# A fused attention and mixture kernel: first products copied by ScalarE into the second's bank, one pooled sum instead of three, and attention, loads and x sums moved in time

## The chip, the cores and the metric

The kernel runs on one core of a Trainium2 chip. A core has a matrix engine (TensorE, "PE" in the profile; its weight loads are "PEld"), a vector engine (DVE), a scalar engine (ScalarE, "ACT"), GpSimd ("POOL") and a sync engine (SP) that mostly issues DMAs. The metric is device time in microseconds (us) of one execution. The kernel before takes 514.0 us in the median of its first three runs (513.14 to 515.52), and the profiled execution spans 511.7 us. All executions quoted here are marked fast. Medians of several chips and sets of runs are quoted, so the ratio to the kernel before, timed in the same rounds, is the number to compare.

## The reference

```python
# attention: batch 8, heads 8, sequence 576, head size 64
k_p, v_p = mean of k, v over groups of 8 tokens              # 72 keys and values
attn = softmax(q @ k_p.T / 8);   attn_out = attn @ v_p
x = attn_out as (8*576, 512)                                  # 4608 tokens
# mixture: 4 experts, hidden size 1024
p = domain_probs / (domain_probs.sum(-1) + 1e-9)
out = sum over e of p[:, e] * (relu(x @ w1[e]) @ w2[e])
```

## The kernel before

The tokens are worked in nine chunks: 512 tokens of each of the eight batches, and one chunk with the remaining 64 of every batch. Chunk 0 is special; it ends near 78 us. Chunks 1 to 8 run in steady state: one expert of a chunk takes seven slots, and each slot holds three products, one of each "unit" of the up projection and one of the down projection of the expert before. Each seven-product scheme computes what eight plain block products would. It pays with sums on DVE: of weights once, of x once per chunk ("x sums", tile xs), of the hidden layer once per expert ("hidden sums", tiles S and H).

Some names in what follows: PSUM is the memory that PE writes its products to; a "bank" here is a tile of 128x512 fp32 in it. A "relu sum" is the DVE instruction that adds a PSUM bank and a copy and takes the relu. xT and kpT are the transposed tokens and the transposed pooled keys, made by DMA transposes. An "x_tok buffer" holds the tokens before their transpose.

```python
# up projection: seven products into two PSUM banks of a unit
bank, grows, lhs, rhs = [
    (0, False, b11, a11),
    (1, False, b21, a12),
    (0, True, t[:, 1], s[:, 1]),
    ...
][step]
...
if step == 0 or step == 3:
    nc.scalar.copy(out=part[:, 0], in_=ps)
elif step == 2:
    nc.scalar.copy(out=part[:, 1], in_=ps)
elif step == 1:
    relu_sum(quarter(0, 0), ps, part[:, 0])        # DVE: relu(PSUM + copy)
elif step == 4:
    relu_sum(quarter(1, 1), ps, part[:, 0])
elif step == 5:
    nc.scalar.activation(out=quarter(0, 1), in_=ps, func=ACT.Relu)
else:
    relu_sum(quarter(1, 0), ps, part[:, 1])

# down projection: each step's block is scaled by a probability and added to acc
if step in pooled and e > 0:                        # pooled = (1, 4, 6)
    for j in range(BLOCKS):
        nc.scalar.activation(out=addend[:, j], in_=ps[:, j], func=ACT.Copy, scale=prob)
    nc.gpsimd.tensor_add(out=dst, in0=dst, in1=addend[:])   # one addend tile only
else:
    for j in range(BLOCKS):
        add(ps[:, j], c, e, row * BLOCKS + j, cols, first)  # DVE, or ScalarE when first

# chunk 0: loads in the GpSimd queue
load_w2(1); load_w1(3); load_w2(2); load_w2(3)
...
# attention of batch b is computed inside chunk b-1: division on DVE into x_tok
# (three buffers), then a DMA transpose x_tok -> xT, then x_sums(b) on DVE
x_tok = npool.tile([P, 2, NPAIR, D], BF16, name="x_tok", bufs=3)
...
put(26, lambda: x_sums(b))
```

The softmax here doesn't subtract the row's maximum and nothing guards it: scores larger than these inputs give would overflow.

Of the kernel before, what the change touches and what calls it, by code (L numbers as in the profile page):

```python
# [10 lines left out]
ALU = mybir.AluOpType  # L11
# [6 lines left out]
def kernel(  # L18
# [54 lines left out]
    wu_bf = wpool.tile([P, E, 3, HK, FH], BF16, name="wu_bf")  # L73
    wt_bf = wpool.tile([P, E, 3, HF, HD], BF16, name="wt_bf")
    acc = const.tile([P, NR, DM], F32, name="acc")
    x_rem = const.tile([P, NPAIR, NT], BF16, name="x_rem")
    ident = const.tile([P, P], BF16, name="ident")
    partial = const.tile([P, 2, 2, NT], F32, name="partial")
# [106 lines left out]
    def combine(dst, a, op, b):  # L185
        nc.vector.tensor_tensor(out=dst, in0=a, in1=b, op=op)  # L186
# [64 lines left out]
    def idle(n):  # L251

        w_ps = work_bank()
        for _ in range(n):
            nc.tensor.matmul(w_ps, lhsT=zeros[:, 0:P], rhs=zeros)  # L255

    def fold_values(b, hs):
        raw = raw_v if b >= BUSY else raws[("vraw", b)]
# [213 lines left out]
    def x_sums(c):  # L472
        a11, a21, a12, a22 = x_parts(c)
        s = state[("xs", c)] = xpool.tile([P, 3, HK, HN], BF16, name="xs")
        combine(s[:, 0], a21, ALU.add, a22)
        combine(s[:, 1], s[:, 0], ALU.subtract, a11)
        combine(a21, a11, ALU.subtract, a21)
        combine(s[:, 2], a12, ALU.subtract, s[:, 1])

    def relu_sum(dst, ps, part):  # L480
        nc.vector._custom_dve(TENSOR_ADD_SAT, out=dst, in0=ps, in1=part, s0=LARGEST, s1=0.0)  # L481
# [1 line left out]
    def up_product(c, e, unit, step):  # L483
        b11, b21, t3, b22 = weight_parts(e)
        a11, s3, a12, a22 = x_parts(c)
        t, s = wu_bf[:, e], state[("xs", c)]
        bank, grows, lhs, rhs = [
            (0, False, b11, a11),
            (1, False, b21, a12),
            (0, True, t[:, 1], s[:, 1]),  # L490
            (0, True, t3, s3),
            (1, False, t[:, 0], s[:, 0]),
            (0, True, t[:, 2], a22),
            (1, True, b22, s[:, 2]),
        ][step]
        ps = units[unit][bank][:]
        for n in range(2):
            for kc in range(HK):
                f = (2 * unit + n) * P
                nc.tensor.matmul(  # L500
                    ps[:, n * HN:(n + 1) * HN], lhsT=lhs[:, kc, f:f + P], rhs=rhs[:, kc, :],
                    start=(not grows and n == 0 and kc == 0), stop=(kc == HK - 1),
                    skip_group_check=True,
                )
        part = partial[:, unit]
        H_sb = hidden[(c, e)]

        def quarter(f, tok):
            return H_sb[:, f, tok, 2 * unit:2 * unit + 2, :].rearrange("p i n -> p (i n)")

        if step == 0 or step == 3:
            nc.scalar.copy(out=part[:, 0], in_=ps)  # L512
        elif step == 2:
            nc.scalar.copy(out=part[:, 1], in_=ps)  # L514
        elif step == 1:
            relu_sum(quarter(0, 0), ps, part[:, 0])
        elif step == 4:
            relu_sum(quarter(1, 1), ps, part[:, 0])
        elif step == 5:
            nc.scalar.activation(out=quarter(0, 1), in_=ps, func=ACT.Relu)  # L520
        else:
            relu_sum(quarter(1, 0), ps, part[:, 1])



# [24 lines left out]
    def down(c, e, step, flip=0, pooled=()):  # L550
# [2 lines left out]
        a11, a12, a21, a22 = quarters(c, e)  # L553
        chain, grows, lhs, rhs, row, col, first = [
            lambda: (0, False, a11, w[:, LO, 0:HD], 0, 0, True),
            lambda: (1, False, a12, w[:, HI, 0:HD], 0, 0, False),
            lambda: (0, True, S2, t[:, 1], 0, 1, True),
            lambda: (1, False, a21, t[:, 0], 1, 1, True),
            lambda: (0, True, S3, w[:, LO, HD:DM], 1, 1, False),
# [10 lines left out]
                    skip_group_check=True,  # L570
                )
        cols = slice(col * HD, (col + 1) * HD)
        if step in pooled and e > 0:
            for j in range(BLOCKS):
                prob = p_all[:, c * NR + row * BLOCKS + j, e:e + 1]
                nc.scalar.activation(out=addend[:, j], in_=ps[:, j], func=ACT.Copy, scale=prob)  # L576
            dst = acc[:, row * BLOCKS:(row + 1) * BLOCKS, cols]
            nc.gpsimd.tensor_add(out=dst, in0=dst, in1=addend[:])  # L578
        else:
            for j in range(BLOCKS):  # L580
                add(ps[:, j], c, e, row * BLOCKS + j, cols, first)
# [78 lines left out]
    make_identity(nc, ident[:])  # L660
    every = slice(0, H)

    def pieces_first():

        at = {}

        def put(s, i, *pieces):
            at.setdefault((s, i), []).extend(pieces)
# [17 lines left out]
        for r in range(NR):  # L686
            put(2, 3 + r, lambda r=r: context(1, r))
            put(2, 4 + r, lambda r=r: turn(1, r))
        put(3, 1, lambda: load_part(2, 1))
        put(3, 3, lambda: load_q(2))  # L690
        put(3, 5, lambda: load_part(2, 2))
        put(3, 7, lambda: x_sums(1))
        return at

    def pieces_at(b):

        at = {}

        def put(slot, piece):
            at.setdefault(slot, []).append(piece)  # L700

        if b < B:
            late = b == BUSY
            put(4 if late else 0, lambda: queries(b))
            put(5 if late else 0, lambda: fold_keys(b, every))
            put(6 if late else 1, lambda: keys(b, every))
            put(7 if late else 5, lambda: fold_values(b, every))
            for pair, slot in enumerate((9, 11, 12, 13) if late else (6, 8, 12, 13)):
                put(slot, lambda pair=pair: scores(b, pair))
            for r in range(NR):  # L710
                put((14, 16, 19, 21)[r], lambda r=r: context(b, r))
                put((15, 17, 20, 22)[r], lambda r=r: turn(b, r))
            put(26, lambda: x_sums(b))
            if late:
                put(1, lambda: load_part(b, 3))
                put(2, lambda: load_q_rem(b))
            if b + 1 < B:
                put(8 if late else 6, lambda: load_part(b + 1, 0))
                put(9 if late else 8, lambda: (load_q(b + 1), load_q_rem(b + 1)))
                put(12, lambda: load_part(b + 1, 1))  # L720
                put(17, lambda: load_part(b + 1, 2))
                put(22, lambda: load_part(b + 1, 3))
        if b % 2 == 0 and b <= B:
            i = b // 2 - 1
            put(0, lambda: rem_queries(i))
            put(4, lambda: rem_scores(i))
            put(7, lambda: rem_context(i))
            put(8, lambda: rem_turn(i))
        if b == B:
            put(12, lambda: x_sums(B))  # L730
        return at

    ENG = mybir.EngineType
    with tc.manual_schedule(
# [11 lines left out]
        load_whole(1, k, "kraw")  # L746
        load_q(1)
        load_whole(1, v, "vraw")
        load_w2(1)
        load_w1(3)  # L750
        load_w2(2)
        load_w2(3)
        load_q_rem(0)
# [1 line left out]
        load_part(2, 0)  # L755

        first_pieces = pieces_first()

        for s, (above, below) in enumerate(
                [((0, 1), None), ((0, 2), (0, 0)), ((0, 3), (0, 1)), (None, (0, 2))]):  # L760
            if s == 1:
                hidden_sums(*below, 0)
                hidden_sums(*below, 1)
            for i in range(FCH):
                if above:
                    up(*above, (i,))
                if below and s != 1 and i % 2:
                    down_plain(*below, i // 2)
                if s == 1 and i < 7:
                    down(*below, i)  # L770
                    if i in (1, 2):
                        hidden_sums(*below, i + 1)
                for piece in first_pieces.get((s, i), ()):
                    piece()
        psum_first.__exit__(None, None, None)
        psum_last = ctx.enter_context(
            tc.tile_pool(name="psum_last", bufs=1, space=bass.MemoryType.PSUM))
        units[0] = [psum_last.tile([P, NT], F32, name=f"unit0{i}") for i in range(2)]



        N = len(order)
        below_of = [(0, 3)] + order
        sums = {}
        for at, pieces in (((2, 3, 4, 5), first_weight_sums(2)), ((9, 10, 12, 13), weight_sums(2)),
                           ((16, 17, 18, 19), first_weight_sums(3))):
            sums.update(zip(at, pieces, strict=True))
        POOLED = (1, 4, 6)
        for g in range(7 * N + 1):
            t, i = divmod(g, 7)  # L790
            if t < N:
                up_product(*order[t], 0, i)
            t2, i2 = divmod(g - 1, 7)
            if 0 <= t2 < N:
                up_product(*order[t2], 1, i2)
            if g >= 1:
                down(*below_of[t2], i2, t2 % 2, POOLED)
            if i < 4 and t < N:
                hidden_sums(*below_of[t], i)
            if t < N:  # L800
                c = order[t][0]
                at = pieces_at(c + 1)
                for piece in at.get(g - 7 * E * (c - 1), ()):
                    piece()
            if g in sums:
                sums[g]()
            if g == 7 * (N - 2):
                load_last_weights()
        down_last(*order[-1])
# [28 lines left out]
```

## Time and profile before

| what | number | where it is read |
|---|---|---|
| PE busy, whole span | 97% of 511.7 us | page, part 1 |
| PE in the chain of waits | 79% | page, part 4 |
| PE busy 150 to 300 us | 149.62 of 150 us | windows |
| PE busy 50 to 60, 80 to 95, 95 to 120, 120 to 150 us | 7.87, 12.97, 22.97, 27.60 us | windows |
| DVE busy 120 to 150 us | 29.03 of 30 us | windows |

The page of the kernel before begins with each engine's busy time, its share of the span and its number of instructions:

```profile
PE 495.1 (97%) x4578; PEld 406.6 (79%) x4578; DVE 405.1 (79%) x776; ACT 291.7 (57%) x557; POOL 181.4 (35%) x160
```

The windows view of the kernel before gives, for each stretch, its length and the busy time of PE, PEld, DVE, ACT and POOL (instructions in brackets), then granted clock, DMA share and GB/s:

```profile
50.00:60.00 10.00, 7.87 (x44) 2.79 (x42) 3.81 (x6) 4.71 (x8) 0.00 (x0) 0.83 1.25 205
80.00:95.00 15.00, 12.97 (x138) 10.46 (x137) 14.24 (x27) 7.82 (x15) 6.10 (x5) 1.00 0.92 112
95.00:120.00 25.00, 22.97 (x223) 19.14 (x222) 22.46 (x44) 15.48 (x28) 11.36 (x10) 1.00 0.80 94
120.00:150.00 30.00, 27.60 (x258) 23.72 (x255) 29.03 (x54) 15.29 (x31) 11.34 (x9) 1.00 0.61 61
150.00:300.00 150.00, 149.62 (x1460) 129.44 (x1460) 127.41 (x247) 93.78 (x179) 68.12 (x56) 1.00 0.72 83
```

The last row is the most important for judging the change: after 150 us PE has nothing to gain. PE's loss between 50 and 150 us shows in the first four rows.

PE's timeline of the kernel before around 54 us (start, duration, what, and in brackets the idle time before it and what ended it):

```profile
51.21 0.39 PE L299 MATMUL att<-qT,kpT 64*128 64x256 bf16 x4
53.73 1.56 PE L448 MATMUL unit<-xT,w_bf 128*128 128x512 bf16 x4 [2.13 <-DMA w_bf<-in_moe_w_dram]
55.22 0.61 PE L299 MATMUL att_first<-qT,kpT 64*128 64x256 bf16 x4
55.76 1.89 PE L448 MATMUL unit<-xT,w_bf 128*128 128x512 bf16 x4
```

PE waits 2.13 us for a weight load. The four matmuls after it take 1.56 and 1.89 us, where the same four take 1.03 us at 50.25 us, at a granted clock of 1.00: the granted clock of the 10 us from 50 to 60 is 0.83 on average, and 0.50 from 54.1 to 57.5 us.

The wait list of the kernel before names what else stops PE later (in total, times, longest):

```profile
PE unit L448 <- DMA w_bf<-in_moe_w_dram: 2.1, 1, 2.1
DVE xs L186 <- DMA xT<-x_tok: 2.1, 2, 1.4
PE att L299 <- DMA kpT<-kp: 2.0, 1, 2.0
PE o_ps L567 <- DVE S L186: 1.6, 3, 1.0
PE unit L500 <- DVE H L481: 1.2, 2, 0.9
```

And the groups that the change touches (line, engine, operation, count, busy us, mean ns of one):

```profile
L481 DVE CUSTOM_DVE_ANT_0 H<-unit,partial 128x512 bf16<-128x512 f32 x192 | 131.4, 684 | 27.2 <-PE unit L500 24.5
L578 POOL TENSOR_TENSOR acc<-acc,addend 128x512 f32<-128x512 f32 x72 | 95.3, 1323 | 256.2 <-ACT addend L576 129.5
```

### The profile page before, as it was taken

How to read it: one execution, taken by the hardware profiler on the slowest of the kernel's cores; microseconds unless marked ns; L12 is line 12 of the kernel's file. 1: busy time of each engine (PE TensorE's matmuls, PEld its weight loads, DVE VectorE, ACT ScalarE, POOL GpSimd, SP SyncE). 2: the span in 40 equal slices, each digit the busy share in tenths (PEclk: the TensorE clock that was granted, in tenths of full speed). 3: DMA queues.
4: the chain of work that ended last, by engine and by line, in shares of the span. 5: the costliest groups of instructions: out<-in, count | busy, mean ns of one | idle time of the engine just before them, and what ended most of it. 6: DMA issues, size and time to landing. Idle time of an engine off the chain costs nothing.

```text
span 511.7 us, 11532 instructions
## 1 busy us (share of the span) xinstructions
PE 495.1 (97%) x4578; PEld 406.6 (79%) x4578; DVE 405.1 (79%) x776; ACT 291.7 (57%) x557; POOL 181.4 (35%) x160
## 2 busy tenths in 40 slices
PE   9999898899899999999999999999999999999995
PEld 4656346688777988798888887888889888888885
DVE  3556388989997998789878986889788879777783
ACT  2675513575457556755575567655855565556550
POOL 6331053426434454435353536353102311222130
PEclk9999899999999999999999999999999999999999
DMA  9999999894929671948194929584111020003003
GB/s 190 210 206 208 189 93 97 144 92 46 76 58 132 54 88 52 140 47 93 35 150 39 99 45 135 56 92 50 63 21 33 21 74 2 0 22 84 1 1 84
DMA packets 106790, 42.51 MB, mean 83 GB/s; under 512 B 79840, under 2 KB 105184, under 8 KB 106736
## 3 DMA queue, kind: packets, MB, share of 16 engines
q0 software_dynamic: 59728, 22.43, 41.9%
q1 hardware_dynamic: 46432, 18.82, 18.8%
q8 instruction: 36, 0.59, 0.5%
q10 hardware_dynamic: 576, 0.52, 0.3%
q14 instruction: 18, 0.15, 0.1%
HBM read 45.69 MB, written 9.44 MB: 108 GB/s over the span
## 4 chain that ended last, share of the span: by engine, by line
PE 79%; DMA 10%; DVE 7%; issue 2%; ACT 1%; POOL 0%; DVEq 0%
PE unit L500 34%; PE o_ps L567 33%; DMA w_bf<-in_moe_w_dram 5%; DMA xT<-x_tok 3%; PE unit L255 2%; PE unit L448 2%; PE att L299 1%; PE unit L619 1%; DVE acc L635 1%; PE o_ps L590 1%; DVE H L481 1%; PE att L325 1%; DVE H L186 1%; DMA kpT<-kp 1%; DVE wu_bf L186 1%
## 5 line engine op out<-in xcount | busy, mean ns | idle before, releaser
L578 POOL TENSOR_TENSOR acc<-acc,addend 128x512 f32<-128x512 f32 x72 | 95.3, 1323 | 256.2 <-ACT addend L576 129.5
L481 DVE CUSTOM_DVE_ANT_0 H<-unit,partial 128x512 bf16<-128x512 f32 x192 | 131.4, 684 | 27.2 <-PE unit L500 24.5
L635 DVE SCALAR_TENSOR_TENSOR acc<-o_ps,p_all,acc 128x256 f32<-128x256 f32 (+1 forms) x254 | 113.2, 486 | 47.2 <-PE o_ps L567 35.0
L567 PEld LDWEIGHTS <-H 128*128 128x128 bf16 x1320 | 129.0, 98 | 17.2 <-DVE H L186 1.2
L500 PEld LDWEIGHTS <-w_bf 128*128 128x128 bf16 x1024 | 96.8, 98 | 17.8 <-issue 6.7
L512 ACT COPY partial<-unit 128x512 f32<-128x512 f32 x128 | 74.9, 585 | 57.0 <-PE unit L500 56.1
L567 PE MATMUL o_ps<-w_bf,H 128*128 128x256 bf16 x792 | 102.6, 273 | 0.0
L500 PE MATMUL unit<-xT,w_bf 128*128 128x256 bf16 x672 | 96.2, 273 | 1.8 <-DVE H L481 1.2
L576 ACT ACTIVATE addend<-o_ps,p_all 128x256 f32<-128x256 f32 x144 | 60.5, 471 | 53.5 <-PE o_ps L567 53.5
L500 PEld LDWEIGHTS <-wu_bf 128*128 128x128 bf16 x768 | 74.2, 98 | 11.2 <-issue 1.3
L500 PE MATMUL unit<-xs,wu_bf 128*128 128x256 bf16 x512 | 76.9, 273 | 0.9 <-DVE xs L186 0.9
L567 PE MATMUL o_ps<-wt_bf,H 128*128 128x256 bf16 x528 | 68.4, 273 | 0.6 <-DVE H L186 0.6
L567 PEld LDWEIGHTS <-S 128*128 128x128 bf16 x528 | 51.4, 98 | 8.8 <-DVE S L186 2.5
L520 ACT ACTIVATE H<-unit 128x512 bf16<-128x512 f32 x64 | 38.2, 596 | 19.0 <-PE unit L500 19.0
L514 ACT COPY partial<-unit 128x512 f32<-128x512 f32 x64 | 38.0, 594 | 18.5 <-PE unit L500 17.8
L500 PE MATMUL unit<-xs,w_bf 128*128 128x256 bf16 x256 | 38.5, 273 | 0.0
L118 POOL DMA_DIRECT2D kraw<-in_k_dram x18 | 25.1, 1396 | 36.2 <-DMA kraw<-in_k_dram 36.2
L303 ACT ACTIVATE expT<-att 72x1024 bf16<-72x1024 f32 x28 | 28.5, 1018 | 15.5 <-PE att L299 15.5
L633 ACT ACTIVATE acc<-o_ps,p_all 128x256 f32<-128x256 f32 x72 | 30.2, 471 | 11.3 <-PE o_ps L567 8.9
L567 PE MATMUL o_ps<-wt_bf,S 128*128 128x256 bf16 x264 | 34.2, 273 | 1.6 <-DVE S L186 1.6
L567 PE MATMUL o_ps<-w_bf,S 128*128 128x256 bf16 x264 | 34.2, 273 | 0.0
L118 POOL DMA_DIRECT2D vraw<-in_v_dram x18 | 33.2, 1845 | 2.1 <-DMA vraw<-in_v_dram 1.9
(106 smaller groups left out, 485.9 us busy)
## 6 DMA issues: line engine op xcount, KB each, us to landing
out_dram<-acc SPq DMA_DIRECT2D x32, 256.0 KB, 2.4
w_bf<-in_moe_w_dram POOLq DMA_DIRECT2D x7, 1024.0 KB, 24.0
q_sb<-in_q_dram POOLq DMA_DIRECT2D x7, 512.0 KB, 10.6
kraw<-in_k_dram POOLq DMA_DIRECT2D x24, 144.0 KB, 6.3
vraw<-in_v_dram POOLq DMA_DIRECT2D x24, 144.0 KB, 7.3
acc<-in_q_dram SPq DMA_DIRECT2D x2, 512.0 KB, 4.6
w_bf<-in_moe_w_dram POOLq DMA_DIRECT2D x2, 512.0 KB, 11.9
wt_bf<-in_k_dram POOLq DMA_DIRECT2D x2, 288.0 KB, 7.1
```

What stands on the lines that cost most here:

```text
L118: nc.gpsimd.dma_start(out=raw[:], in_=rows, accum_op=ALU.add)
L303: nc.scalar.activation(out=expT[:, 2 * pair:2 * pair + 2].rearrange("j h a b t -> j b (h a) t"), in_=sc_ps[0:SP].rearrange("j b h (a t) -> ...
L481: nc.vector._custom_dve(TENSOR_ADD_SAT, out=dst, in0=ps, in1=part, s0=LARGEST, s1=0.0)
L500: nc.tensor.matmul(ps[:, n * HN:(n + 1) * HN], lhsT=lhs[:, kc, f:f + P], rhs=rhs[:, kc, :], start=(not grows and n == 0 and kc == 0), stop ...
L512: nc.scalar.copy(out=part[:, 0], in_=ps)
L514: nc.scalar.copy(out=part[:, 1], in_=ps)
L520: nc.scalar.activation(out=quarter(0, 1), in_=ps, func=ACT.Relu)
L567: nc.tensor.matmul(ps[:, j], lhsT=lhs[:, i, j * P:(j + 1) * P], rhs=rhs[:, i, :], start=(not grows and i == 0 and j == 0), stop=(i == HF - 1),
L576: nc.scalar.activation(out=addend[:, j], in_=ps[:, j], func=ACT.Copy, scale=prob)
L578: nc.gpsimd.tensor_add(out=dst, in0=dst, in1=addend[:])
L633: nc.scalar.activation(out=dst, in_=o_ps, func=ACT.Copy, scale=prob)
L635: nc.vector.scalar_tensor_tensor(out=dst, in0=o_ps, scalar=prob, in1=dst, op0=ALU.mult, op1=ALU.add,)
```

## The change

The intent is to take work from DVE and to keep what arrives late from stopping PE. Product 0 of a unit is copied by ScalarE from its PSUM bank into the other bank, and product 1 accumulates on the copy in PE, so its relu needs no addition and moves to ScalarE. The down product does the same, so step 0 needs no add of its own. Two of three pooled steps go back to DVE. In time: the w1 load of expert 3 goes ahead of w2 of expert 1; loads of batch 2 wait behind a "gate" (a tiny GpSimd copy that reads xT) until xT of batch 1 has landed; attention of batch 2 goes later into chunk 1, that of later batches begins four slots earlier, at the end of the chunk before; the x sums are spread over slots; hidden sums are queued earlier in their slot. Weight sums and some plain down products of chunk 0 change slots too.

The two `open_bank` matmuls each write one target bank (`chains[1]` and `units[0][1]`) once before the first copy into it.

The diff, cut to its core (parts are left out between the pieces):

```diff
+    def open_bank(ps):
+        nc.tensor.matmul(ps, lhsT=ident[:], rhs=w2_bf[:, 0, 0, :], skip_group_check=True)
 # up product
-            (1, False, b21, a12),
+            (1, True, b21, a12),
-        if step == 0 or step == 3:
-            nc.scalar.copy(out=part[:, 0], in_=ps)
-        elif step == 2:
-            nc.scalar.copy(out=part[:, 1], in_=ps)
+        if step == 0:
+            nc.scalar.copy(out=units[unit][1][:], in_=ps)
+        elif step == 2 or step == 3:
+            nc.scalar.copy(out=part[:, step - 2], in_=ps)
         elif step == 1:
-            relu_sum(quarter(0, 0), ps, part[:, 0])
+            nc.scalar.activation(out=quarter(0, 0), in_=ps, func=ACT.Relu)
 # down product
-            lambda: (1, False, a12, w[:, HI, 0:HD], 0, 0, False),
+            lambda: (1, True, a12, w[:, HI, 0:HD], 0, 0, True),
+        if step == 0:
+            nc.scalar.copy(out=chains[(1 + flip) % 2][:], in_=chains[flip][:])
-        POOLED = (1, 4, 6)
+        POOLED = (4,)
 # loads and slots
+        load_w1(3)
         load_w2(1)
-        load_w1(3)
-        put(3, 1, lambda: load_part(2, 1))
+        put(3, 1, gate, lambda: load_part(2, 1))
 ... (attention, loads and x sums by slot; of batch 2:)
+    (4, 10, (14, 15, 16, 17), (18, 19, 20, 22), (12, 14, 13, 16, 19)) if b == 2
+    for n, slot in enumerate((24, 25, 25, 26) if b == 2 else (16, 16, 20, 23) if b < B
 # hidden sums ahead of the up product instead of behind the down product
+            if i in (0, 2, 3) and t < N:
+                hidden_sums(*below_of[t], i)
 ... (i == 1: behind the up products)
```

More of the change, by code (lines that the diff above doesn't have):

```diff
@@ L75 @@
     acc = const.tile([P, NR, DM], F32, name="acc")
+    gate_at = const.tile([1, NR], BF16, name="gate")
     x_rem = const.tile([P, NPAIR, NT], BF16, name="x_rem")
@@ L474, in x_sums, with x_sum @@
         s = state[("xs", c)] = xpool.tile([P, 3, HK, HN], BF16, name="xs")
-        combine(s[:, 0], a21, ALU.add, a22)
-        combine(s[:, 1], s[:, 0], ALU.subtract, a11)
-        combine(a21, a11, ALU.subtract, a21)
-        combine(s[:, 2], a12, ALU.subtract, s[:, 1])
+        return [lambda: combine(s[:, 0], a21, ALU.add, a22),
+                lambda: combine(s[:, 1], s[:, 0], ALU.subtract, a11),
+                lambda: combine(a21, a11, ALU.subtract, a21),
+                lambda: combine(s[:, 2], a12, ALU.subtract, s[:, 1])]
+    def x_sum(c, n):
+        if n == 0:
+            state[("x_sums", c)] = x_sums(c)
+        state[("x_sums", c)][n]()
     def relu_sum(dst, ps, part):
@@ L509, in quarter @@
             return H_sb[:, f, tok, 2 * unit:2 * unit + 2, :].rearrange("p i n -> p (i n)")
-        if step == 0 or step == 3:
-            nc.scalar.copy(out=part[:, 0], in_=ps)
-        elif step == 2:
-            nc.scalar.copy(out=part[:, 1], in_=ps)
+        if step == 0:
+            nc.scalar.copy(out=units[unit][1][:], in_=ps)
+        elif step == 2 or step == 3:
+            nc.scalar.copy(out=part[:, step - 2], in_=ps)
         elif step == 1:
-            relu_sum(quarter(0, 0), ps, part[:, 0])
+            nc.scalar.activation(out=quarter(0, 0), in_=ps, func=ACT.Relu)
         elif step == 4:
-            relu_sum(quarter(1, 1), ps, part[:, 0])
+            relu_sum(quarter(1, 1), ps, part[:, 1])
         elif step == 5:
@@ L521, in up_product @@
         else:
-            relu_sum(quarter(1, 0), ps, part[:, 1])
+            relu_sum(quarter(1, 0), ps, part[:, 0])
     def weight_sums(e):
@@ L572, in down @@
         cols = slice(col * HD, (col + 1) * HD)
-        if step in pooled and e > 0:
+        if step == 0:
+            nc.scalar.copy(out=chains[(1 + flip) % 2][:], in_=chains[flip][:])
+        elif step in pooled and e > 0:
             for j in range(BLOCKS):
@@ L661, with gate @@
     every = slice(0, H)
+    def gate():
+        nc.gpsimd.tensor_copy(out=gate_at[:], in_=state[("xT", 1)][0:1, 0, 0:NT:P])
     def pieces_first():
@@ L688, in pieces_first, with pieces_later @@
             put(2, 4 + r, lambda r=r: turn(1, r))
-        put(3, 1, lambda: load_part(2, 1))
-        put(3, 3, lambda: load_q(2))
-        put(3, 5, lambda: load_part(2, 2))
-        put(3, 7, lambda: x_sums(1))
+        put(3, 1, gate, lambda: load_part(2, 1))
+        put(3, 2, lambda: load_q(2))
+        put(3, 4, lambda: load_part(2, 2))
+        put(3, 6, lambda: load_part(2, 3), lambda: load_q_rem(2))
+        put(3, 7, *(lambda n=n: x_sum(1, n) for n in range(4)))
         return at
-    def pieces_at(b):
+    def pieces_later():
@@ L697, in pieces_at @@
         at = {}
-        def put(slot, piece):
-            at.setdefault(slot, []).append(piece)
-        if b < B:
-            late = b == BUSY
-            put(4 if late else 0, lambda: queries(b))
-            put(5 if late else 0, lambda: fold_keys(b, every))
-            put(6 if late else 1, lambda: keys(b, every))
-            put(7 if late else 5, lambda: fold_values(b, every))
-            for pair, slot in enumerate((9, 11, 12, 13) if late else (6, 8, 12, 13)):
-                put(slot, lambda pair=pair: scores(b, pair))
-            for r in range(NR):
-                put((14, 16, 19, 21)[r], lambda r=r: context(b, r))
-                put((15, 17, 20, 22)[r], lambda r=r: turn(b, r))
-            put(26, lambda: x_sums(b))
-            if late:
-                put(1, lambda: load_part(b, 3))
-                put(2, lambda: load_q_rem(b))
-            if b + 1 < B:
-                put(8 if late else 6, lambda: load_part(b + 1, 0))
-                put(9 if late else 8, lambda: (load_q(b + 1), load_q_rem(b + 1)))
-                put(12, lambda: load_part(b + 1, 1))
-                put(17, lambda: load_part(b + 1, 2))
-                put(22, lambda: load_part(b + 1, 3))
@@ L723, in pieces_at, with put @@
-        if b % 2 == 0 and b <= B:
-            i = b // 2 - 1
-            put(0, lambda: rem_queries(i))
-            put(4, lambda: rem_scores(i))
-            put(7, lambda: rem_context(i))
-            put(8, lambda: rem_turn(i))
-        if b == B:
-            put(12, lambda: x_sums(B))
+        def put(slot, *pieces):
+            at.setdefault(slot, []).extend(pieces)
+        for b in range(2, B + 1):
+            start = 7 * E * (b - 2)
+            if b < B:
+                q_at, k_at, scores_at, contexts_at, loads_at = (
+                    (4, 10, (14, 15, 16, 17), (18, 19, 20, 22), (12, 14, 13, 16, 19)) if b == 2
+                    else (-4, -4, (3, 4, 5, 6), (8, 9, 11, 13), (-2, 17, 0, 3, 6)))
+                put(start + q_at, lambda b=b: queries(b))
+                put(start + k_at, lambda b=b: fold_keys(b, every))
+                put(start + k_at + 1, lambda b=b: keys(b, every), lambda b=b: fold_values(b, every))
+                for pair, slot in enumerate(scores_at):
+                    put(start + slot, lambda b=b, pair=pair: scores(b, pair))
+                for r, slot in enumerate(contexts_at):
+                    put(start + slot, lambda b=b, r=r: context(b, r))
+                    put(start + slot + 1, lambda b=b, r=r: turn(b, r))
+            if b + 1 < B:
+                first, q_too, *others = loads_at
+                put(start + first, lambda b=b: load_part(b + 1, 0))
+                put(start + q_too, lambda b=b: load_q(b + 1), lambda b=b: load_q_rem(b + 1))
+                for part, slot in enumerate(others):
+                    put(start + slot, lambda b=b, part=part: load_part(b + 1, part + 1))
+            if b % 2 == 0:
+                i = b // 2 - 1
+                put(start if b == 2 else start - 3, lambda i=i: rem_queries(i))
+                put(start + (5 if b == 2 else 16), lambda i=i: rem_scores(i))
+                put(start + (9 if b == 2 else 18), lambda i=i: rem_context(i))
+                put(start + (10 if b == 2 else 19), lambda i=i: rem_turn(i))
+            for n, slot in enumerate((24, 25, 25, 26) if b == 2 else (16, 16, 20, 23) if b < B
+                                     else (23, 24, 24, 25)):
+                put(start + slot, lambda b=b, n=n: x_sum(b, n))
@@ L757 @@
         first_pieces = pieces_first()
+        plain_at = {(2, 2): 0, (2, 4): 1, (2, 6): 2, (2, 7): 3}
+        plain_at.update({(3, 2 * r + 1): r for r in range(NR - 1)})
         for s, (above, below) in enumerate(
@@ L761 @@
             if s == 1:
+                open_bank(chains[1][:])
                 hidden_sums(*below, 0)
@@ L766 @@
                     up(*above, (i,))
-                if below and s != 1 and i % 2:
-                    down_plain(*below, i // 2)
+                if (s, i) in plain_at:
+                    down_plain(*below, plain_at[s, i])
                 if s == 1 and i < 7:
@@ L778 @@
         units[0] = [psum_last.tile([P, NT], F32, name=f"unit0{i}") for i in range(2)]
+        open_bank(units[0][1][:])
         N = len(order)
+        later = pieces_later()
         below_of = [(0, 3)] + order
         sums = {}
-        for at, pieces in (((2, 3, 4, 5), first_weight_sums(2)), ((9, 10, 12, 13), weight_sums(2)),
-                           ((16, 17, 18, 19), first_weight_sums(3))):
-            sums.update(zip(at, pieces, strict=True))
-        POOLED = (1, 4, 6)
+        for at, pieces in (((2, 2, 3, 4), first_weight_sums(2)), ((14, 14, 16, 16), weight_sums(2)),
+                           ((9, 9, 10, 13), first_weight_sums(3))):
+            for slot, piece in zip(at, pieces, strict=True):
+                sums.setdefault(slot, []).append(piece)
+        POOLED = (4,)
         for g in range(7 * N + 1):
             t, i = divmod(g, 7)
+            if i in (0, 2, 3) and t < N:
+                hidden_sums(*below_of[t], i)
             if t < N:
@@ L795 @@
                 up_product(*order[t2], 1, i2)
-            if g >= 1:
-                down(*below_of[t2], i2, t2 % 2, POOLED)
-            if i < 4 and t < N:
-                hidden_sums(*below_of[t], i)
-            if t < N:
-                c = order[t][0]
-                at = pieces_at(c + 1)
-                for piece in at.get(g - 7 * E * (c - 1), ()):
-                    piece()
-            if g in sums:
-                sums[g]()
+            if i == 1 and t < N:
+                hidden_sums(*below_of[t], i)
+            if g == 0:
+                down_plain(0, 2, NR - 1)
+            else:
+                down(*below_of[t2], i2, t2 % 2, POOLED)
+            for piece in later.get(g, ()):
+                piece()
+            for piece in sums.get(g, ()):
+                piece()
             if g == 7 * (N - 2):
```

## The prediction

Two passages on the hardware that no trace of this case shows are cut from the recorded text, and the cuts are marked. The gains named, 3.6 + 1.1 + 2.2 + 1.6 + 3.05 + 1.5 (3.05 is the sum of the waits at 125 to 146 us), come to about 13 us, the costs, 1 to 2 + 1 + 0.4, to about 3 us, and with 514 us these give the 503.8. The 1.4 us of slow matmuls are read from the trace of the kernel before (granted clock 0.50 from 54.1 to 57.5 us). That a copy into PSUM takes the 0.585 us of the copies into SBUF was the assumption.

> **What bounds it now.** TensorE. The page gives PE 97% of 511.7 us, PE heads 79% of the chain of waits, and in the windows view PE is busy 49.87 to 50 of every 50 us from 150 to 500 us. The timeline there shows four 128x256 matmuls every 0.44 us without a break; start-to-start excess over the usual pitch, summed from 150 us on, is only about 1.2 us. So all DVE relief after 150 us is worth almost nothing. Only 0 to 150 us can shrink: excess about 4 us before 50 us (the change doesn't touch it) and about 11.7 us from 50 to 150 us.
>
> **What the change moves.**
> - The w1 load of expert 3 goes before w2 of expert 1. In the trace they land at 53.68 and 48.73 us; swapped, w1 lands near 48.7. That removes the 2.13 us PE wait at 53.7 and the slow matmuls after it (about 427 instead of 216 ns pitch, granted clock 0.83 in 50 to 60 us, about 1.4 us). [...] Gain 3.6 us.
> - Part loads of batch 2 held back until xT of batch 1 landed (its transposes took 8.84 us beside them, 2.4 alone): the 1.1 us wait for xs at 81.7 goes.
> - Keys of batch 2 at slot 10, scores from 14: the 2.2 us wait for kpT at 100.4 goes.
> - Step 0 of each product is copied by ScalarE to the other bank; step 1 accumulates on it. DVE loses 64 relu sums (0.68 us each, about 44 us in all), ScalarE gains 64 relus (0.60, 38 us). In the down product step 0 needs no add; two of three pooled steps return to DVE. Estimate: DVE 405 to about 375 us, POOL 181 to about 120, ScalarE 292 to about 305. Waits on DVE between 80 and 95 us (S2, a21, H; about 1.6) and 125 to 146 us (1.17, 1.07, 0.34, 0.47) mostly go, as DVE is busy 46.5 of 50 us in 100 to 150 now.
> - Copies of step 2 to their own buffer: six waits of 0.29 us on ScalarE go, up to 1.5 us.
> Together about 13 us at most.
>
> **What comes back.** PE now waits for a copy between step 0 and step 1. In the down product only two 0.44 us products stand between. ScalarE starts 0.20 us after PE's next issue, takes 0.585, PE resumes 0.05 later: 0.84 against 0.87. It fits, barely[...]. Exp (1.02 us) ahead of a copy falls mostly in slots with slack. I allow 1 to 2 us here, and 1 us for DVE in chunk 1, still about 95% full. Two bank-opening matmuls: 0.4 us.
>
> **Prediction.** 514 - 13 + 3 = about 503.8 us, range 501 to 508. Faster by over 2%: 0.53; within: 0.46; slower: 0.01.
>
> **What would show it.** Chain of waits: no wait for w1 near 51 us, clock about 1.0 in 50 to 60. Wait list: no PE wait on kpT, xs, S; PE-busy 100 to 150 us from 47.2 to over 49. Groups: new copy unit<-unit, 64 of about 0.58 us, o_ps<-o_ps, 33; relu sums 192 to 128; pooled adds 72 to 24. Step 1 matmuls show few waits on ScalarE, under 0.1 us each.
>
> **What would make it wrong.** PSUM-to-PSUM copies much slower than 0.6 us: 33 down steps would each stall PE by the excess. w2 of expert 1 landing too late (53.7 us, wanted near 54.9). Batch 2's third and fourth part landing after slot 10 and holding DVE. Either leaves 505 to 509.

## The result

The changed kernel takes 506.81 us in the median (505.88 to 508.39, four runs), the kernel before 513.57 us in the same rounds (four runs). The ratio is 0.9865, with a 95% interval of 0.9827 to 0.9902. A ratio is computed as the mean time of one kernel's fast runs over that of the other's of the same rounds, so it is not quite the ratio of the medians quoted. The gain is 6.8 us of the 9.8 us predicted (513.6 - 503.8), and the verdict is within 2%, where the prediction had put 0.46, against 0.53 for faster.

Part 1 of the page of the changed kernel:

```profile
PE 492.7 (98%) x4572; PEld 406.9 (81%) x4580; DVE 377.4 (75%) x742; ACT 300.5 (60%) x558; POOL 119.9 (24%) x113
```

The estimates of the engines' load (DVE about 375, ScalarE about 305, POOL about 120) hold. The same windows as before:

```profile
50.00:60.00 10.00, 9.95 (x70) 4.34 (x70) 6.23 (x10) 7.62 (x13) 0.00 (x0) 1.00 1.26 205
80.00:95.00 15.00, 15.00 (x163) 13.09 (x162) 14.58 (x27) 9.53 (x19) 6.04 (x5) 1.00 1.28 173
95.00:120.00 25.00, 24.98 (x253) 21.07 (x252) 23.20 (x48) 17.55 (x32) 13.06 (x11) 1.00 1.11 89
120.00:150.00 30.00, 27.46 (x259) 22.64 (x258) 23.36 (x46) 17.95 (x32) 13.43 (x11) 1.00 0.81 95
150.00:300.00 150.00, 149.39 (x1443) 129.05 (x1442) 118.95 (x234) 95.66 (x179) 40.10 (x35) 1.00 0.66 79
```

Everything from 50 to 120 us was gained: PE is full, and the clock is 1.00. But from 120 to 150 us PE loses as much as before (27.46 busy against 27.60), although DVE is now 23.36 us busy there instead of 29.03. DVE isn't overfull; something else holds it. Over 100 to 150 us PE is busy 47.44 us, against 47.22 before and the "over 49" of the prediction. The groups of the copies and of what was spared:

```profile
L491 DVE CUSTOM_DVE_ANT_0 H<-unit,partial 128x512 bf16<-128x512 f32 x128 | 87.6, 685 | 23.2 <-PE unit L510 16.9
L523 ACT COPY unit<-unit 128x512 f32<-128x512 f32 x64 | 37.2, 582 | 30.9 <-PE unit L510 26.1 <-DVE H L491 4.1 <-PE o_ps L578 0.7
L586 ACT COPY o_ps<-o_ps 128x512 f32<-128x512 f32 x33 | 18.8, 570 | 4.6 <-PE o_ps L578 3.2 <-DVE acc L649 0.9 <-DVE S L187 0.3
```

The copies take 582 and 570 ns, as costed (585). The last two groups also show the new coupling: a ScalarE copy sometimes waits for DVE, and PE waits for the copy.

What holds DVE at 120 to 132 us is in its timeline, and what that does to PE in PE's. DVE of the changed kernel:

```profile
121.67 0.88 DVE L649 SCALAR_TENSOR_TENSOR acc<-o_ps,p_all,acc 128x256 f32<-128x256 f32 x2 [0.20 <-PE o_ps L578]
125.28 0.42 DVE L187 TENSOR_TENSOR xs<-xT 128x512 bf16<-128x512 bf16 x1 [2.73 <-DMA xT<-x_tok]
125.62 0.75 DVE L221 TENSOR_TENSOR kp<-kraw 72x512 bf16<-72x512 bf16 x2
126.29 0.68 DVE L491 CUSTOM_DVE_ANT_0 H<-unit,partial 128x512 bf16<-128x512 f32 x1
```

PE of the changed kernel:

```profile
124.08 1.04 PE L578 MATMUL o_ps<-w_bf,S 128*128 128x256 bf16 x8
127.02 0.60 PE L510 MATMUL unit<-xs,w_bf 128*128 128x256 bf16 x4 [1.90 <-DVE H L491]
...
131.48 0.70 PE L510 MATMUL unit<-xT,w_bf 128*128 128x256 bf16 x5 [0.60 <-ACT unit L523]
```

The n-th relu of product 5 (ScalarE) can be set side by side in both profiles, to see where the gain arises. The changed kernel is 9.1 us ahead at the relu that comes at 106 us in the kernel before (96.91 against 106.04), 7.0 us ahead at that of 135 us (128.09 against 135.13), and 7.3 us at the end. So all was gained by 106 us, and 2.1 us of it was lost by 135 us.

The first x sum of batch 2 stands in DVE's queue while its input, a DMA transpose, is still under way. The relu sum behind it could have run. PE needs the bank that this relu sum empties, so it waits 1.90 us, and some more behind it.

A second small loss is new. A timeline of several engines of the changed kernel near 196 to 201 us:

```profile
196.42 2.50 DVE L187 TENSOR_TENSOR S<-H 128x1024 bf16<-128x1024 bf16 x1
196.53 1.83 POOL L592 TENSOR_TENSOR acc<-acc,addend 128x512 f32<-128x512 f32 x1
...
199.44 0.86 DVE L649 SCALAR_TENSOR_TENSOR acc<-o_ps,p_all,acc 128x256 f32<-128x256 f32 x2
...
200.39 0.57 ACT L586 COPY o_ps<-o_ps 128x512 f32<-128x512 f32 x1 [0.21 <-DVE acc L649]
...
201.01 0.27 PE L578 MATMUL o_ps<-w_bf,H 128*128 128x256 bf16 x1 [0.19 <-ACT o_ps L586]
```

A hidden sum of usually 0.68 us takes 2.50 us beside a GpSimd add. DVE comes late to the add that empties a bank, the ScalarE copy into that bank waits for it, and PE waits for the copy.

To count such losses we use PE's start-to-start excess: how much later each matmul starts than the median distance behind the same kind of matmul, summed. (Missing matmul records, which look like an excess of one pitch, are taken out by hand.) By it the changed kernel loses about 3.2 us between 127 and 135 us, and about 2.0 us in all in waits for the copies at 106, 161, 200, 253, 306 and 372 us. The prediction had 1 us for the first and 1 to 2 us for the second.

### The profile page after: what moved, and what is told of

It is laid out like the page before. It is cut to its first block, busy times and chain, and to the rows that moved or that the text cites. A ratio compares the mean times of both kernels' runs of the same rounds, so it can differ in the third digit from the quotient of the medians.

```text
span 504.4 us, 11269 instructions
## 1 busy us (share of the span) xinstructions
PE 492.7 (98%) x4572; PEld 406.9 (81%) x4580; DVE 377.4 (75%) x742; ACT 300.5 (60%) x558; POOL 119.9 (24%) x113
## 4 chain that ended last, share of the span: by engine, by line
PE 87%; DVE 5%; DMA 5%; ACT 1%; issue 1%; DVEq 0%; POOL 0%; ACTq 0%; POOLq 0%
PE o_ps L578 36%; PE unit L510 35%; PE unit L453 5%; DMA xT<-x_tok 3%; PE o_ps L604 3%; DVE S L187 2%; PE att L304 2%; DVE acc L649 2%; DMA wt_bf<-in_k_dram 2%; PE unit L633 1%; DVE H L491 1%; PE att L330 1%; PE unit L240 1%; PE unit L256 1%; ACT o_ps L586 0%
## 5 line engine op out<-in xcount | busy, mean ns | idle before, releaser
L649 DVE SCALAR_TENSOR_TENSOR acc<-o_ps,p_all,acc 128x256 f32<-128x256 f32 (+1 forms) x284 | 126.3, 485 | 58.0 <-PE o_ps L578 40.1
L510 PEld LDWEIGHTS <-w_bf 128*128 128x128 bf16 x1024 | 98.0, 98 | 18.0 <-issue 6.4
L491 DVE CUSTOM_DVE_ANT_0 H<-unit,partial 128x512 bf16<-128x512 f32 x128 | 87.6, 685 | 23.2 <-PE unit L510 16.9
L592 POOL TENSOR_TENSOR acc<-acc,addend 128x512 f32<-128x512 f32 x24 | 34.0, 1415 | 263.3 <-ACT addend L590 255.2
L525 ACT COPY partial<-unit 128x512 f32<-128x512 f32 x128 | 72.0, 590 | 31.3 <-PE unit L510 30.8
L510 PEld LDWEIGHTS <-wu_bf 128*128 128x128 bf16 x768 | 73.1, 98 | 10.8 <-issue 2.5
L523 ACT COPY unit<-unit 128x512 f32<-128x512 f32 x64 | 37.2, 582 | 30.9 <-PE unit L510 26.1
L531 ACT ACTIVATE H<-unit 128x512 bf16<-128x512 f32 x64 | 38.1, 596 | 29.3 <-PE unit L510 29.0
L527 ACT ACTIVATE H<-unit 128x512 bf16<-128x512 f32 x64 | 38.8, 606 | 27.6 <-PE unit L510 27.6
L510 PE MATMUL unit<-xT,wu_bf 128*128 128x256 bf16 x224 | 33.7, 273 | 0.0
```

The costliest lines, as they stand in the source:

```text
L491: nc.vector._custom_dve(TENSOR_ADD_SAT, out=dst, in0=ps, in1=part, s0=LARGEST, s1=0.0)
L510: nc.tensor.matmul(ps[:, n * HN:(n + 1) * HN], lhsT=lhs[:, kc, f:f + P], rhs=rhs[:, kc, :], start=(not grows and n == 0 and kc == 0), stop ...
L523: nc.scalar.copy(out=units[unit][1][:], in_=ps)
L525: nc.scalar.copy(out=part[:, step - 2], in_=ps)
L527: nc.scalar.activation(out=quarter(0, 0), in_=ps, func=ACT.Relu)
L649: nc.vector.scalar_tensor_tensor(out=dst, in0=o_ps, scalar=prob, in1=dst, op0=ALU.mult, op1=ALU.add,)
```

## The experiments

Twelve kernels, each timed in five rounds. All outputs are right.

### 1. The x sums of batch 2 one or two slots later

```diff
-            for n, slot in enumerate((24, 25, 25, 26) if b == 2 else ...
+            for n, slot in enumerate((26, 26, 27, 27) if b == 2 else ...
```

> The changed kernel, with the four x sums of batch 2 at slots 26, 26, 27, 27 instead of 24, 25, 25, 26. Theory: the largest wait that the change left (PE waits 2.07 us excess at 127.0 us, 0.21 at 129.4, 0.76 at 131.5, 0.15 at 134.3, 3.2 us in all) comes from the in-order DVE standing idle 2.73 us at the first x sum until the last transpose of xT lands at 125.18 us. Then 506.8 goes to about 503.6 us, and the DVE's wait on xT and PE's waits near 127 to 134 us are gone. Rival: the DVE is simply overfull in chunk 1; then the wait shows up a few us later and the time moves under 1 us.

Measured: 504.39 us median, ratio 0.9824 (0.9792 to 0.9855). The wait is gone; the windows row of 120 to 150 us now has PE full:

```profile
120.00:150.00 30.00, 30.00 (x288) 25.47 (x286) 25.38 (x50) 20.65 (x37) 14.25 (x12) 1.00 0.94 108
```

So the cause of the largest remaining loss is shown: the order in DVE's queue, not DVE's load. The time fell by 2.4 us in the medians rather than 3.2, and the two ratios' intervals (0.9827 to 0.9902 for the changed kernel) still overlap a little. The profiled run shows where the rest went: a wait of 0.9 us at 98 us, some 5 us after a hidden sum that took 2.91 us beside a GpSimd add of 1.86 (that this sum caused it is argued, not shown), and one of 0.9 us excess at 160 us, where DVE's division had waited 1.32 us for an x_tok buffer.

### 2. No pooled step at all

```diff
-        POOLED = (4,)
+        POOLED = ()
```

> The changed kernel without the last pooled step (DVE adds step 4 too). Theory: the waits of 0.2 to 0.35 us for the ScalarE copies at 200, 253 and 306 us come from DVE work slowed beside GpSimd's add (a hidden sum took 2.50 us instead of 0.68 while GpSimd's add took 1.83), which holds the drain that the copy waits for. Then those waits go (about 1.5 us), DVE busy rises from 377 to about 395 us, and the time falls by up to 1.5 us unless chunk 1 gets fuller. Rival: the ScalarE queue is too full after the exps; then the waits at 200, 253, 306 us stay as they are and the time is the same or longer.

Measured: 504.27 us, ratio 0.9819 (0.9795 to 0.9844). DVE takes on more adds, and the kernel isn't slower for it but about as fast as experiment 1. The waits at 200, 253 and 306 us are gone, and no hidden or weight sum takes over 1.0 us any more. The x sum wait remains (PE 28.77 of 30 us in 120 to 150), and this profile has a new wait of 1.25 us at 213 us, where the division waited 1.82 us for an x_tok buffer. GpSimd's help was worth nothing here. That dropping it makes the changed kernel faster is not clear of noise by this run alone: the intervals (0.9795 to 0.9844 and 0.9827 to 0.9902) overlap a little.

That the sums are lengthened by GpSimd is not only this one example. Counted over the traces, every one of DVE's 128x1024 sums over 1.0 us overlaps a GpSimd add: 10 of 10 in the kernel before, 5 of 5 in the changed one, none without pooled steps. In the changed kernel the five that overlap take 2.21 us on average, the other 159 take 0.68. Each of these fifteen long sums ends 0.55 to 0.56 us after the add that it overlaps: none of them ended before its add did. Not every overlap is long: in the kernel before 23 sums overlap an add and 10 take over 1.0 us. DVE instructions with one input in PSUM are no longer beside an add in the changed kernel: relu sums take 0.69 us beside one and 0.68 otherwise, scale-and-adds (128x256) 0.48 and 0.48. Why the sums of two SBUF tiles are held up and these are not, no run shows.

### 3. The load order alone, on the kernel before

```diff
-        load_w2(1)
         load_w1(3)
+        load_w2(1)
```

> The kernel before, with the w1 load of expert 3 ahead of the w2 load of expert 1 and nothing else. Theory: the PE wait of 2.13 us at 53.7 us and the slow-clock matmuls after it go, 3.6 us: 513.6 to about 510.0 us, granted clock 1.00 in 50 to 60 us. Rival: the wait is handed to the w2 load, wanted only 2 us later, or the earlier PE is stopped at 72 to 82 us by the transposes of xT, unmoved beside the loads: under 1.5 us gained.

Measured: 511.63 us against 513.66, ratio 0.9957 (0.9934 to 0.998), so about 2.2 us, not 3.6. The wait at 53.7 us and its slow clock are gone. The gain is there at first: followed instruction by instruction (DVE and ScalarE run the same ones in the same order in both kernels), this profile is 3.7 us ahead of the kernel before from 60 to 78 us. It is still ahead by that much when PE's wait for kpT ends, at 96.70 us against 100.37, as kpT also lands earlier. Behind this wait PE is slow, and from 106 us on the lead is about 2.0 us. PE's timeline of this experiment:

```profile
96.70 0.39 PE L299 MATMUL att<-qT,kpT 64*128 64x256 bf16 x4 [2.35 <-DMA kpT<-kp]
...
98.04 1.91 PE L567 MATMUL o_ps<-wt_bf,S 128*128 128x256 bf16 x8
99.75 1.06 PE L500 MATMUL unit<-xs,wu_bf 128*128 128x256 bf16 x4
```

Eight matmuls that usually take 1.04 us take 1.91, and the page's granted clock is under 0.9 in the slice from 89 to 102 us. This slow clock, about 1.7 us of excess up to 101 us, was not there in the kernel before, whose wait for kpT was 2.0 us (granted clock 1.00 from 97.6 to 120 us). So what took the gain back in this profile is the slow clock and not later data. PE's wait for xs, 0.94 us at 81.7 us in the kernel before, is gone too, with the load order alone.

### 4. The copies and one pooled step alone, on the kernel before

Its edit is the up and down parts of the diff above, `open_bank` and `POOLED`; loads and slots as before.

> The kernel before, with the ScalarE copies into the second bank, the two bank-opening matmuls and one pooled step, but the loads and the slots of before. Theory: DVE busy falls from 405 to about 377 us, but only the waits on DVE in 80 to 146 us (about 4.6 us in all) can shrink, so 2 to 4 us are gained: about 510.5 us. Rival: DVE relief is worth nothing there as the DVE stands behind xT and kpT transposes, not behind its own work: 513 us or above, with the added waits for copies.

Measured: 510.50 us, ratio 0.9932 (0.9909 to 0.9955), so about 3.5 us by the ratio. PE's losses from 120 to 150 us shrink from about 3.2 to about 1.0 us of excess, but the wait for kpT grows to 3.50 us, and behind it eight matmuls again take 1.91 us instead of 1.04. The theory's size holds.

### 5. The copies undone in the changed kernel

```diff
 (up product, down product and open_bank as in the kernel before)
-        POOLED = (4,)
+        POOLED = (1, 4, 6)
```

> The changed kernel without its copies, bank-opening matmuls and with three pooled steps, as before; loads and slots as changed. Theory: with DVE back near 405 us its waits in chunk 1 are longer than with the copies, by 2 to 4 us: about 509.5 us; the waits on copies after 150 us go. Rival: the slots and loads alone hold the whole gain: 506.8 or less.

Measured: 513.82 us, ratio 1.0008 (0.9977 to 1.004). Loads and slots without the copies give nothing at all, far worse than expected; the rival is out. DVE is busier than in either kernel:

```profile
PE 494.8 (97%) x4570; PEld 407.0 (80%) x4578; DVE 439.4 (86%) x776; ACT 290.3 (57%) x557; POOL 182.9 (36%) x161
L187 DVE TENSOR_TENSOR H<-H,S 128x1024 bf16<-128x1024 bf16 x33 | 40.3, 1220 | 0.0
L187 DVE TENSOR_TENSOR S<-H,S 128x1024 bf16<-128x1024 bf16 x33 | 39.3, 1191 | 0.1
```

The earlier hidden sums of the new order meet GpSimd's adds: 38 sums over 1.0 us, all beside an add, 45 us above their usual time. This was the natural suspect, and experiment 6 tested it.

### 6. The same, with the hidden sums back in their old order

```diff
-            if i in (0, 2, 3) and t < N:
-                hidden_sums(*below_of[t], i)
 ...
                 down(*below_of[t2], i2, t2 % 2, POOLED)
+            if i < 4 and t < N:
+                hidden_sums(*below_of[t], i)
```

> The kernel with the copies undone, and its hidden sums also back in the order of before (after the down product). Theory: copies_undone lost its gain because the earlier hidden sums met GpSimd's adds (38 sums over 1.0 us, 45 us of excess, DVE busy 439 us). In the order of before there are some 10 such sums, DVE is back near 405 us, and the time is 509 to 511 us, as the new load order still gives its 2 to 3.6 us. Rival: the new slots themselves overload DVE without the copies: 513 us again.

Measured: 513.51 us, ratio 0.9989 (0.9952 to 1.0025). The long sums fall from 38 to 15 and DVE's busy time from 439 to 414 us, but the time doesn't move. So the 45 us of slowed sums were not what cost the gain; the theory fell. Its profiled run is the fastest of six (509.44 us) and can't stand for the median, but it shows one thing that experiments 5 and 7 show too, and which the next experiment settles.

### 7. The changed kernel, copies kept, with three pooled steps

```diff
-        POOLED = (4,)
+        POOLED = (1, 4, 6)
```

> The changed kernel, copies kept, with three pooled steps (1, 4, 6) as before instead of one. DVE is spared about 37 us of adds on paper. Theory: the DVE's two-input sums of 128x1024 wait beside GpSimd's adds (all 10 sums over 1.0 us in the kernel before overlap one, all 5 in the changed kernel, all 38 with the copies undone, none without pooled steps), so more pooled steps slow DVE's sums and the copies that wait on DVE: over 10 such sums, and 1 to 5 us slower than the changed kernel. Rival: DVE load is what counts: DVE falls to about 345 us and the time is the same or less.

Measured: 510.09 us, ratio 0.9933 (0.9906 to 0.996): about 3.5 us slower than the changed kernel by the ratios, with DVE at 350 us instead of 377. The two intervals don't meet. The theory's numbers hold (13 long sums, 1 to 5 us slower), but most of the loss has another cause than the one given. Three engines of this experiment near 90 us:

```profile
84.11 1.38 POOL L119 DMA_DIRECT2D kraw<-in_k_dram  x1 [3.07 <-DMA kraw<-in_k_dram]
...
87.42 1.84 POOL L592 TENSOR_TENSOR acc<-acc,addend 128x512 f32<-128x512 f32 x1
89.30 0.84 ACT L590 ACTIVATE addend<-o_ps,p_all 128x256 f32<-128x256 f32 x2 [5.63 <-POOL acc L592]
90.19 1.76 PE L578 MATMUL o_ps<-wt_bf,H 128*128 128x256 bf16 x8 [2.77 <-ACT addend L590]
```

GpSimd's queue is in order too. The first pooled add, whose addend was ready near 80 us, starts at 87.42 us, behind part loads of batch 2, each of which waits for the one before it to land (3.07 us ahead of the load at 84.11, 0.38 ahead of that at 85.87). There is only one addend tile, so ScalarE can't take the next step, its bank stays full, and PE waits 2.77 us, with a slow clock behind it (the eight matmuls take 1.76 us instead of 1.04; the granted clock is 0.89 from 80 to 95 us). Experiments 5 and 6 have the same wait, 3.2 and 2.8 us in their wait lists. With one pooled step per expert the next one comes seven slots later, and the changed kernel has no such wait. So, by these traces, the cut in pooled steps is what lets the new load slots pay. No run tried it the other way, with a second addend tile or later part loads.

### 8. The load order undone in the changed kernel

The diff of experiment 3 in reverse.

> The changed kernel with only the load order put back (w2 of expert 1 before w1 of expert 3). Theory: the PE wait of 2.1 us at 53.7 us and the 1.4 us of half-clock matmuls after it come back, and as nothing behind them has slack in this kernel, the time rises by 3.6 us to about 510 us. Rival: as in the load order alone, only 2 us.

Measured: 508.68 us, ratio 0.9901 (0.9872 to 0.9931): by the ratios about 1.8 us slower than the changed kernel, not 3.6. The intervals (0.9872 to 0.9931 and 0.9827 to 0.9902) overlap, so this run alone excludes neither 0 nor 3.6 us. The profiled run is by far the slowest of its seven (515.09 us) and can't stand for the median; at its place the load order costs what was predicted (ScalarE falls back 3.6 us against the changed kernel between 51 and 60 us). Experiment 3 gives 2.2 us in all, of 3.7 us at its place. What makes the total of experiment 8 smaller than 3.6 us stays open.

### 9. Without the gate

```diff
-        put(3, 1, gate, lambda: load_part(2, 1))
+        put(3, 1, lambda: load_part(2, 1))
```

> The changed kernel without the GpSimd copy that holds the loads of batch 2 until xT of batch 1 has landed. Theory: the last transposes of batch 1 then share the DMA engines with those loads, land some us later than 70.9 us, and PE or DVE waits for xs or xT at 72 to 78 us: 0.5 to 2 us slower than the changed kernel. Rival: the w2 loads that end near 64 us were what slowed the transposes before, and the gate is worth nothing: within 0.5 us.

Measured: 507.24 us, ratio 0.9877 (0.9835 to 0.9918). The last transpose of batch 1 does land later, at 74.23 us instead of 70.87, but no PE or DVE wait on it appears at 72 to 78 us. The rival holds: no worth of the gate is shown (0.6 us in the ratio, well inside the interval). The prediction had credited the gate with the 1.1 us wait for xs; experiment 3 has no gate and no such wait.

### 10 to 12. Putting the remedies together

```diff
 (x_late_four)     experiment 1, and  name="x_tok", bufs=4
 (x_late_no_pool)  experiments 1 and 2
 (all_three)       experiments 1 and 2, and  name="x_tok", bufs=4
```

> The changed kernel with the x sums of batch 2 late (26, 26, 27, 27) and four x_tok buffers instead of three. Theory: of what x_late left after 150 us (waits of PE on the ScalarE copies of 0.92 us at 160, 0.52 at 266, 0.34 at 305), the cause is that the division writing x_tok for the fourth block waits for the first block's transpose to read its buffer (DVE idle 1.32 and 0.92 us there), the relu sum behind it comes late, and the copy into the bank it reads waits. With a fourth buffer the DVE's wait x_tok on xT goes to about 0 and these waits go: about 1.5 us under x_late, so some 503 us. Rival: the waits come from ScalarE's own queue: DVE's wait goes, PE's waits stay, time as x_late.

> The changed kernel with the late x sums of batch 2 and no pooled step, but three x_tok buffers. Theory: the fourth buffer matters, as DVE's division waits for it (up to 1.82 us, PE 1.4 us at 213 us in no_pool): 502.5 to 503.5 us, 0.7 to 1.7 above the kernel with all three. Rival: without GpSimd's adds the loads go out earlier and the transposes land in time: as with all three, 501.8 us.

> The same, and no pooled step. Theory: the three causes (x sums behind xT, x_tok buffers, GpSimd beside DVE) are separate, so their gains add: PE's excess after 50 us falls from about 5.2 in the changed kernel to about 1 us, a median of 501.5 to 502.5 us. Rival: without GpSimd's help DVE (about 395 us) is the limit in chunk 1, and the waits come back there: 503.5 or more.

| kernel | median us | ratio to before | 95% interval |
|---|---|---|---|
| changed kernel | 506.81 | 0.9865 | 0.9827 to 0.9902 |
| x sums late, four buffers | 505.02 | 0.9846 | 0.9809 to 0.9882 |
| x sums late, no pooled step | 502.66 | 0.9785 | 0.9758 to 0.9812 |
| all three | 501.79 | 0.9775 | 0.9745 to 0.9805 |

The fourth buffer alone didn't help, against the theory's 503 us. DVE no longer waits to write x_tok, but then stands 3.3 us at the x sum of batch 3 until the same transposes land, and PE waits 2.2 us; the granted clock of 150 to 300 us is 0.99, and under 0.9 in the page's slice from 164 to 177 us. The wait moved from the buffer to the data. The last two rows, without and with a fourth buffer, don't differ beyond their intervals, so the theory that the fourth buffer matters isn't borne out. All three together came out as expected (501.79 us, of 501.5 to 502.5). Late x sums and no pooled step together are faster than the changed kernel beyond doubt (the intervals don't meet), and faster than the kernel before by about 11 us. The windows of "all three":

```profile
120.00:150.00 30.00, 29.29 (x278) 24.41 (x277) 24.88 (x53) 18.73 (x32) 11.64 (x10) 1.00 1.03 118
150.00:300.00 150.00, 150.00 (x1457) 130.06 (x1455) 123.96 (x256) 89.35 (x160) 31.97 (x27) 1.00 0.72 78
```

After 50 us PE is full but for 0.7 us in 120 to 150. Since the fourth buffer shows no gain, the simplest version that beats both kernels is the one with the x sums late and no pooled step.

## Why the prediction was right, and where its sizes were off

The measured 506.8 us lies in the range of 501 to 508, 1.2 us from its upper end. The point, 503.8, was 3.0 us too low, and the likelier class by the prediction (faster by over 2%, 0.53) did not come; that the range held is in part luck.

The step that failed is the stretch of 120 to 150 us. Up to 105 us the prediction counted 3.5 + 1.1 + 2.2 + 1.6 = 8.4 us of waits to go, and the changed kernel is 9.1 us ahead at 106 us. From 125 to 146 us it counted another 3.05 us to gain, less 1 us; instead 2.1 us were lost.

- **PE bounds the kernel and only 0 to 150 us can shrink: right.** The changed kernel gained nothing after 150 us (PE 149.39 of 150 against 149.62), though DVE's load fell by 28 us.
- **Waits at 54, 80 to 95 and 100 us go: right.** PE is full in these stretches. The wait for kpT goes with the new slots: experiments 3 and 4, with the old ones, still have it (2.35 and 3.50 us), experiments 5 to 7 don't. The reason given for one part was wrong: the wait for xs isn't cured by the gate (experiment 9).
- **Loads of the engines: right.** DVE 377, ScalarE 300, POOL 120 us. Copies take 0.57 to 0.58 us and fit between the products in most slots.
- **"1 us for DVE in chunk 1, still about 95% full": this term was mis-sized.** It measured about 3.2 us, at 127 to 135 us. Chunk 1 wasn't limited by how full DVE was (23.36 of 30 us in 120 to 150). It was limited by an x sum that the change itself put two slots earlier in DVE's queue, before its transpose could land; experiment 1 removed it by moving four instructions back by one or two slots.
- **"Gain 3.6 us" for the load order: right at its place**, 3.7 us in the profile of experiment 3. Taken alone it is worth 2.2 us in all, as in that profile a slow clock behind the wait for kpT takes the rest (eight matmuls in 1.91 us instead of 1.04). The changed kernel has no wait for kpT.
- **"1 to 2 us" for copies: right**, about 2.0 us. The cause was only half seen. The copy's own time (0.57 to 0.58 us) fits; it loses when DVE, delayed beside GpSimd's add or behind a transpose, empties the target bank late (the copies waited 4.1 us for relu sums and 0.9 us for adds of DVE in all, by the groups above).
- **"Up to 1.5 us" for step 2's own buffer: not seen as a gain.** PE no longer waits for the copies into `partial`, but it now waits for the new ones; from 135 us to the end the lead grows only from 7.0 to 7.3 us.
- **Parts of a change don't add.** The copies with one pooled step gain 3.5 us alone, the load order 2.2 us alone, loads and slots with everything else undone 0. In experiments 3 and 4 the wait for kpT remains, with slow matmuls behind it (1.91 us for eight) that neither the kernel before nor the changed one has there.

## What to carry to other kernels

Here the first instruction in DVE's queue that wasn't ready stopped those behind it (DVE 2.73 us, and PE 1.90 us after it), so place an instruction that waits for a DMA by when its data lands, not by when there is room. Before giving a small sum to GpSimd, look for two things in the trace: whether DVE's sums of two SBUF tiles are longer beside it (here 2.21 us on average instead of 0.68), and what DMA issues stand ahead of it in its queue (here they held an add for 7.4 us). When a wait is removed alone, look at the next wait: in experiment 3 a slow clock behind it (eight matmuls in 1.91 us instead of 1.04) took 1.7 of the 3.7 us gained.

## What the traces here show in numbers

- A sum of two 128x1024 bf16 tiles on DVE goes from 0.68 us to 2.21 us on average (longest 2.57) beside a GpSimd add in the changed kernel, and DVE's relu sums, with one PSUM input, don't change (0.69 and 0.68 us).
- In the kernel before, PE's granted clock falls to 0.50 once between 7 us and the last 0.3 us: from 54.10 to 57.52 us, 3.41 us, after the wait of 2.13 us. It stays at 1.00 after its wait of 2.0 us for kpT and after the wait of 1.90 us in the changed kernel. In experiments 3, 7 and 4, after waits of 2.35, 2.77 and 3.50 us, eight matmuls take 1.91, 1.76 and 1.91 us instead of 1.04. What decides whether the clock falls isn't shown; no run tested it.
- In the kernel before and the changed one, a 128x512 fp32 copy by ScalarE from PSUM takes 570 to 582 ns into PSUM and 585 to 594 ns into SBUF, so the difference is small.
- A DMA transpose of a 128x512 bf16 tile landed in about 2.4 us at best, and with other loads in flight in up to 9.0 us (kernel before); the one that held the x sum in the changed kernel took from 119.32 to 125.18 us.
